# A fused attention and mixture-of-experts kernel: the g column by two matmuls, fewer unused matmuls, a new emission order

## The chip, the cores and the metric

One core of a Trainium2 chip runs the whole program. The metric is the device time of one execution in microseconds. A core has five engines with queues of their own: TensorE (PE in the rows, its weight loads PEld), VectorE (DVE), ScalarE (ACT), GpSimd (POOL) and SyncE (SP). DMAs are issued from SP and POOL here.

## What is computed

Linear attention without softmax for 8 batches of 8 heads, 576 positions and 64 columns, a root-mean-square norm over the 64 columns, and a layer of 8 experts of which each batch takes one, chosen by the mean over its positions:

```python
kv = np.einsum('bhsd,bhse->bhde', k, v)
out = np.einsum('bhsd,bhde->bhse', q, kv)
rms = np.sqrt(np.mean(out * out, axis=-1, keepdims=True) + 1e-06)
x = out / rms * g_norm            # then heads side by side: (8, 576, 512)
...
logits = x.mean(axis=1) @ w_gate  # (8, 8)
e_idx = np.argmax(logits, axis=1)
...
h = np.maximum(x[mask] @ w1[e], 0.0)                     # 512 -> 1024
out[mask] = gate_w[mask, None, None] * (h @ w2[e])       # 1024 -> 512
```

The inputs are the same in every run; the experts drawn are 4, 4, 7, 6, 5, 1, 3, 1 for the batches 0 to 7.

## The kernel before

Every step is a small function, and one long string, `ORDER`, names all steps in the order in which they are emitted: two letters, the batch, then arguments (`m1031` is `m1(0, 3, 1)`). Each engine and each DMA queue executes its instructions in this order and waits at each for its operands; so the string fixes who stands behind whom on every engine. Nothing is rescheduled.

Per batch the steps are these. `lq`, `lk`, `lv` load q, k and v (POOL, converted to f16 on the way; q of batch 0 comes over SP in f32 and is converted by `cq`). `kv` multiplies k and v on TensorE (L230), `kc` and `ks` copy the result. q is transposed by `tr` and `te` (TensorE and a VectorE copy, batches 0 and 1) or by `td` (VectorE, batches 2 to 7). `ou` (batches 0 and 1, L278) and `op` (L265) multiply q with kv, for four groups c, each the even or the odd columns of four heads. `oc` copies the product, `sq` squares it, `sa` adds two squares, `me` sums over the 64 columns with a matmul of ones (L322, L327), `ln` takes the reciprocal root (L334), and `xt` (VectorE, L342) writes x in f16, transposed, times the g column `gcol`, with the sum over the positions as a by-product. `ga` and `gb` (batch 0: `gd`, L369) give the logits, `gc` takes their maximum and its index on VectorE (L382). `g2` (POOL) and `g3` give the gate weight.

The weights of the chosen expert are kept in three slots for w1 and three for w2. `cw` first copies the slot that holds the expert if an earlier batch chose it; `wl` and `wm` (POOL queue) then load w1 and w2 only if no earlier one did. For batch 0 the first half of w1 is loaded in f32 by four DMAs on the SP queue (`wh`, L440), as soon as the index is known, and converted by `wc` (L447); `wl01` loads the other half. The expert itself is sixteen blocks `m1` (L488, four matmuls of 288 columns each) with the relu `re` behind each, five tiles `m2` (L508, L516), the scaling `ev` and the stores `so` (SP).

`du` emits so many matmuls of zeros whose result nobody reads (L351). `ph1` changes the PSUM pools from three double banks and two single ones to two double and four single ones. `cs` sets up the constants. `sg4` makes SP wait for the index of batch 4.

Of the kernel before, what the change touches and what calls it, by code (L numbers as in the profile page):

```python
# [25 lines left out]
wl1 m1050 sq23 re050 m1070 oc231 m1020 re070 m1071 re071 re020 m1021 op20 oc20 sq20 sa201 re021
oc221 m1151 re151 td31 m1171 re171 m1141 m1161 sq22 re161 lv5 lq40 lk4 me20 m1170 re170 m1130
re130 lv4 m1030 ln20 sa211 m1100 re100 m1131 re131 me21 ln21 re030 re141 td30 m1111 kv31 kv30
xt20 xt22 xt23 m1121 re121 kc3 ks30 m1140 re140 xt21 ga2 ks311 cw12 m1150 re150 m1101 re101
m1160 re160 op30 oc301 m1110 re110 oc321 sq32 sq301 gb2 gc2 cw21 g30 m203 op31 sq31 ev031 oc311  # L30
re111 m1120 m202 m200 g21 sq33 sa311 oc33 wl2 sa30 me30 du2 lk5 ev02 ev00 ln30 m201 me31 re120
wm1 cw22 xt30 kv41 ln31 g31 xt31 xt33 m204 ev041 ev011 m211 ev111 kv40 m214 ev141 lq41 xt32 ga3
gb3 gc3 cw31 m213 ev131 m1200 re200 m1241 re241 kc4 ks40 ks411 m1230 kv51 m1201 re201 m1240 td40
re240 m1270 td41 re270 m1210 re210 re230 m1271 m1261 re271 kv50 kc5 ks501 m1250 op40 oc401 sq40
re261 oc42 sq421 m212 ev12 m1221 m1211 re221 re250 op41 sq41 lq50 g22 lq51 td51 sa401 m210 ks511
wl3 m1321 oc41 m1370 me40 oc431 sq431 sa411 td50 re211 re321 re370 m1330 ln40 xt40 m1331 re331
me41 ln41 re330 m1220 m1260 re260 xt43 xt41 re220 op50 m1231 sq52 oc521 xt42 ga4 m1371 re371
m1310 re310 lv6 re231 lk6 kv61 ev101 so10 wm2 oc50 m1340 sq50 gb4 m1320 gc4 lq60 cw41 lq61 kv60
re340 kc6 m1251 re251 m1301 re301 op51 sq51 re320 oc511 sq53 oc53 wl4 cw32 m1311 re311 td61
m1350 re350 g32 m1300 re300 td60 ks61 m223 m1361 re361 sa50 m1351 re351 me50 m1341 re341 m1360  # L40
re360 ln50 xt50 ev23 sa51 me51 ln51 xt52 m220 m224 ev24 ks601 op60 sq60 m222 sq62 oc621 ev22 wm3
ev20 m221 xt51 ev21 so24 oc601 m1451 m1431 op61 re431 xt53 m1411 re411 re451 m1400 re400 oc61
lk7 g23 g33 sq611 sq63 oc63 m1410 m1471 re410 re471 m1430 re430 m232 lv7 g24 ev321 cw42 ga5
m1441 re441 m1470 re470 gb5 m1440 re440 m1420 lq70 lq71 m1401 sa601 me60 ln60 re401 gc5 cw51
re420 m233 ev331 sa611 me61 ln61 kv70 td70 xt62 kv71 kc7 ks71 td71 m1461 re461 g34 so31 m1421
m1460 m1450 re450 re460 m231 re421 xt61 xt63 so01 m230 ks701 ev301 op71 sq71 so04 oc711 so14 wm4
m234 sq73 oc731 m240 op70 oc701 cw52 ev311 ev341 xt60 ga6 sq70 m243 sq72 gb6 ev40 gc6 m242 wl5
m1540 wm5 sa71 ev421 ev431 m241 cw61 sa701 m1541 re541 me70 re540 wl6 ev41 m1501 oc72 m1560
re501 re560 m1571 m1561 re571 m1510 re510 m1550 re550 re561 m1570 m1511 re511 m1520 m1531 re531
m1551 me71 so41 re520 re570 so40 re551 ln70 m1530 m1521 re521 cw62 wm6 m244 m254 re530 ln71 ev44  # L50
m253 g25 g35 ev531 m1500 m1641 re500 re641 so30 m1620 re620 m1661 ev541 so21 so54 re661 m1600
re600 m250 ev501 m1621 re621 xt72 xt71 xt73 xt70 ga7 m1671 re671 gb7 gc7 so11 so00 m1631 m1640
re631 m1630 re630 m1651 re651 m1670 so34 re670 m1601 re601 m252 ev521 re640 m1660 m251 ev511
so20 so50 re660 cw71 wl7 m1741 re741 m1650 re650 m1730 m1761 re761 m1611 re611 m1751 re751 so51
m1700 re700 m1770 cw72 wm7 re730 m1610 re610 re770 m1750 m1721 re721 g26 g36 m1771 re771 m1731
re731 m1710 re710 m1711 m1701 re711 re701 re750 m1760 re760 m1720 re720 m1740 g27 g37 m262 m260
ev60 ev62 m274 m264 m261 ev74 ev61 re740 m271 ev64 so64 so60 so74 m263 ev711 ev631 so61 m272
# [545 lines left out]
```

## Time and profile before

| | |
|---|---|
| three runs | 192.07, 193.81, 194.74 us; median 193.81 |
| profiled execution | 194.13 us, span 192.2 us |
| mean granted TensorE clock | 0.973 |
| TensorE / VectorE / ScalarE / GpSimd busy | 176.0 / 107.9 / 109.0 / 51.7 us |
| DMA | 37.64 MB, mean 196 GB/s |

The span runs from the first to the last instruction; the time of the execution holds 1.9 us more. Busy time is the time in which at least one instruction of the engine runs. In the clock strip one digit stands for 4.8 us and 9 for the full clock of 2.4 GHz. In the windows the columns are the stretch, its length, the busy time of PE, PEld, DVE, ACT and POOL with the number of instructions begun, the granted clock, the mean share of the 16 DMA engines that is busy, and what they wrote in GB/s. A bracket in the timeline says how long the engine had been idle and what ended that.

### The profile page before, as it was taken

The page shows a single profiled execution, that of the slowest core. Times are in us where ns is not written, and L with a number is a line of the kernel's source. Part 1 is how long each engine was busy: PE and PEld are TensorE (multiplying, and loading weights), DVE is VectorE, ACT ScalarE, POOL GpSimd, SP SyncE. Part 2 cuts the span into 40 slices and gives each one's busy share as a digit, 9 for nine tenths or more (in the row PEclk, how much of TensorE's full clock was granted, in tenths as well). Part 3 has the DMA queues.
Part 4 walks back from the last instruction along what each step waited for, and adds up shares of the span by engine and source line. Part 5 has one row for each costly group of instructions (what it writes and reads, how often), then busy time and mean ns, then how long its engine had stood idle before and what let it go on. Part 6 is the DMA issues. An engine that isn't in the chain of part 4 may idle for free.

```text
span 192.2 us, 5276 instructions
## 1 busy us (share of the span) xinstructions
PE 176.0 (92%) x2189; PEld 105.1 (55%) x2189; DVE 107.9 (56%) x229; ACT 109.0 (57%) x241; POOL 51.7 (27%) x68
## 2 busy tenths in 40 slices
PE   7937999789999899999999999979699999999994
PEld 2424435356675355756566466644377575775452
DVE  1135563787798594769949997487433615003211
ACT  2525202789888633979897555665367554880120
POOL 7630029400900750800056901101215004200000
PEclk9995599999999999999999999999999999999999
DMA  5899989999999699899999999999999996600085
GB/s 198 154 212 206 208 151 169 240 207 208 216 204 205 90 204 206 132 205 207 211 234 201 164 202 207 212 258 274 219 211 219 308 284 260 222 0 3 14 314 193
DMA packets 24071, 37.64 MB, mean 196 GB/s; under 512 B 1904, under 2 KB 15984, under 8 KB 23920
## 3 DMA queue, kind: packets, MB, share of 16 engines
q0 software_dynamic: 16992, 25.63, 76.6%
q1 hardware_dynamic: 7056, 11.69, 17.7%
q8 instruction: 17, 0.28, 0.5%
q14 instruction: 6, 0.05, 0.1%
HBM read 61.88 MB, written 9.44 MB: 371 GB/s over the span
## 4 chain that ended last, share of the span: by engine, by line
PE 45%; DMA 29%; ACT 8%; issue 7%; DVE 6%; SPq 1%; POOL 1%; DVEq 0%; POOLq 0%
DMA w<-in_moe_w_dram 18%; PE ps_m L488 17%; PE ps_m L508 17%; DMA vt<-in_v_dram 5%; DMA qf<-in_moe_w_dram 5%; PE ps_d L351 3%; ACT sq L302 2%; ACT hT L496 2%; PE ps_a L230 2%; PE ps_m L516 2%; DVE w L406 2%; PE ps_a L265 1%; ACT ln L334 1%; DVE xT L342 1%; PE ps_a L327 1%
## 5 line engine op out<-in xcount | busy, mean ns | idle before, releaser
L488 PE MATMUL ps_m<-xT,w 128*128 128x288 f16 x512 | 70.2, 286 | 2.6 <-DMA w<-in_moe_w_dram 1.6
L508 PE MATMUL ps_m<-w,hT 128*128 128x512 f16 (+1 forms) x264 | 59.2, 373 | 2.4 <-DMA w<-in_moe_w_dram 1.2
L488 PEld LDWEIGHTS <-w 128*128 128x128 f16 x512 | 48.8, 98 | 19.7 <-issue 2.9
L496 ACT ACTIVATE hT<-ps_m 128x288 f16<-128x288 f32 x128 | 48.3, 419 | 14.9 <-PE ps_m L488 12.6
L508 PEld LDWEIGHTS <-hT 128*128 128x128 f16 x264 | 25.2, 99 | 29.5 <-issue 4.2
L521 ACT ACTIVATE ot<-ps_m,gates 128x512 f32<-128x512 f32 (+1 forms) x19 | 12.8, 677 | 27.2 <-PE ps_m L508 25.3
L342 DVE SCALAR_TENSOR_TENSOR xT<-o,gcol,ln 128x576 f16<-128x576 f32 x32 | 24.8, 808 | 2.1 <-ACT o L308 1.0
L406 DVE COPY w<-w 128x4096 f16 (+1 forms) x14 | 18.4, 1318 | 11.1 <-DMA w<-in_moe_w_dram 6.4
L523 DVE TENSOR_SCALAR ot<-ps_m,gates 128x512 f32<-128x512 f32 (+1 forms) x14 | 9.9, 727 | 20.4 <-PE ps_m L508 19.7
L432 POOL DMA_DIRECT2D w<-in_moe_w_dram x7 | 3.7, 530 | 64.9 <-DMA w<-in_moe_w_dram 22.9
L302 ACT ACTIVATE sq<-ps_a 128x576 f32<-128x576 f32 (+1 forms) x26 | 16.7, 661 | 5.8 <-DVE o L308 2.5
L351 PE MATMUL ps_d<-junk 128*128 128x512 f16 x47 | 17.2, 479 | 2.1 <-DVE eps L165 1.3
L215 DVE STREAM_TRANSPOSE qT<-qt 128x1152 f16<-128x1152 f16 x12 | 16.2, 1365 | 2.8 <-DMA qt<-in_q_dram 2.7
L308 DVE COPY o<-ps_a 128x576 f32<-128x576 f32 x14 | 10.5, 753 | 11.6 <-ACT sq L302 8.2
L334 ACT ACTIVATE ln<-ps_a,eps 128x576 f32<-128x576 f32 x16 | 11.8, 744 | 5.7 <-PE ps_a L322 4.5
L351 PEld LDWEIGHTS <-junk 128*128 128x128 f16 x63 | 6.6, 116 | 12.9 <-issue 9.2
L469 POOL TENSOR_TENSOR lg<-e,lg 128x8 f32<-128x8 f32 x8 | 13.5, 1688 | 0.1
L242 ACT CAST kv<-ps_a 128x256 f16<-128x256 f32 x9 | 3.3, 372 | 16.9 <-issue 11.1
L308 ACT COPY o<-ps_a 128x576 f32<-128x576 f32 x18 | 11.7, 648 | 2.1 <-PE ps_a L265 2.0
L463 POOL DMA_DIRECT2D w<-in_moe_w_dram x8 | 4.7, 587 | 24.8 <-DVE w L406 10.4
L230 PE MATMUL ps_a<-vt,kt 64*64 64x64 f16 x648 | 7.9, 199 | 3.3 <-DMA vt<-in_v_dram 3.3
L230 PEld LDWEIGHTS <-kt 64*64 64x64 f16 x648 | 6.7, 112 | 6.1 <-issue 5.5
(64 smaller groups left out, 135.3 us busy)
## 6 DMA issues: line engine op xcount, KB each, us to landing
w<-in_moe_w_dram POOLq DMA_DIRECT2D x15, 1024.0 KB, 11.5
...
```

The source lines that it names most:

```text
L215: nc.vector.transpose(s["qT"][:, js].rearrange("p j a n -> p (j a n)"), s["q"][:, js].rearrange("p j d -> p (j d)"))
L230: nc.tensor.matmul(pk[64 * o:64 * o + 64, i, c * Dh:(c + 1) * Dh], s["k"][rs, cc, j, :], s["v"][rs, cc, j, :], start=(j == 0), stop=(j == 8))
L302: nc.scalar.activation(t, po, AF.Square)
L308: (nc.scalar.copy if act else nc.vector.tensor_copy)(t, po)
L334: nc.scalar.activation(t.rearrange("p (i n) -> p i n", i=2), s["pm", C][:, :, 0:HS], AF.Abs_reciprocal_sqrt, bias=cs["eps"])
L342: nc.vector.scalar_tensor_tensor(out=s["xT"][:, c, :], in0=s["o", c], scalar=cs["gcol"][:, c % 2:c % 2 + 1], in1=s["ln", c // 2], op0=ALU. ...
L351: nc.tensor.matmul(t, cs["junk"][:, 0:P], cs["junk"], start=True, stop=True)
L406: nc.vector.tensor_copy(w[:, b % 3:b % 3 + 1, :], w[:, ds(s["src"], 1), :])
L469: nc.gpsimd.tensor_tensor(out=s["lg"], in0=cs["e"], in1=s["lg"], op=ALU.pow)
L488: nc.tensor.matmul(ph[:, 0:HS], w1[:, c, c0:c0 + 255:2], s["xT"][:, c, i * HS:(i + 1) * HS], start=(c == 0), stop=(c == NC - 1))
L496: nc.scalar.activation(s["hT"][:, f, i * HS:(i + 1) * HS], s["ph", f, i][:, 0:HS], AF.Relu)
L508: nc.tensor.matmul(po[:, ds_], s["hT"][:, f, c0:c0 + P], s["w2"][:, f, ds_], start=(f == 0), stop=(f == 7))
```

## The change

The g vector, which four DMAs wrote as a column into four groups of 32 partitions, is loaded as one row, four times side by side on one partition; the new step `cg` makes the column from it with two matmuls against a single 1.0 and a VectorE copy. The string ORDER is new from end to end. It holds one block of 16 unused matmuls at the start, ten more between batch 1's kv products and the first expert matmul, one at the end, and none elsewhere; before there were 19 at the start, 37 more up to the first expert matmul, 2 later and 5 at the end. A number of `oc`, `sq`, `sa`, `ks` and `ev` steps change their engine. Both strings are shown up to batch 1's logits, and at their end.

```diff
 ORDER = """
-lk00 lq0 cq01 du1 du2 du16 cs tr02 wg cq00 tr00 lv00 tr01 te00 kv00 du2 te01 kc00 ou01 ou00 sq00
-oc00 lk01 oc011 lv01 kv01 kc01 ou02 sq011 me00 sq02 oc02 ln00 xt00 ou03 sq03 xt01 me01 ln01
-oc031 xt03 gd00 du2 xt02 du2 du2 gd01 du2 du2 du2 gd03 gd02 lq1 du2 du2 du2 gc0 lq21 du2 du1 du1
-du2 du2 ph1 lv1 tr11 lq20 td20 tr12 tr10 td21 lk1 kv11 kv10 te11 lv2 du2 du1 kc1 te10 ou10 oc10
-ou13 du2 sq10 ou12 sq13 oc13 wh00 wc002 oc121 du2 sq121 sa111 wh01 wh10 wc102 wc0241 du2 ou11
-oc111 sq11 sa101 m1010 m1001 wh11 wc1241 wb me11 re001 ln11 xt13 re010 m1000 me10 ln10 m1031
-re031 m1011 re000 wl01 m1061 re061 lk2 m1041 re041 xt10 xt11 xt12 ga1 lq30 m1060 re060 g20 lk3
-lq31 kv21 kv20 kc2 ks20 ks211 m1051 re051 gb1 gc1 cw11 m1040 re040 lv3 re011 wm0 op21 sq21 oc21
...
-ev721 sg4 so72 so71 so44 m270 ev70 so70 m273 ev73 so73 m275 ev751 cw01 du2 du1 du2 so75
+lq0 cs wg lk00 du16 cq01 cq00 tr02 te01 cg tr00 tr01 te00 lv00 kv00 kc00 ou01 oc011 ou00 sq011
+sq00 me00 ln00 lk01 lv01 kv01 kc01 ou02 oc001 xt00 sq02 xt01 oc02 lq1 ou03 sq03 oc031 me01 ln01
+xt03 gd03 gd01 gd00 xt02 gd02 gc0 ph1 tr11 lv1 tr10 te10 tr12 te11 lk1 kv11 kv10 du2 kc1 ou10
+oc101 sq10 lq21 lq20 td20 lv2 ou12 wh00 wh01 lk2 oc12 sq121 du2 wh10 ou13 sq13 oc131 du1 ou11
+sa111 me11 g20 wl01 oc11 sq11 du2 sa10 du1 wc002 lv3 td21 wc0241 ln11 xt13 xt12 du2 m1001 me10
+wc102 m1011 re001 ln10 re011 xt11 wh11 wc1241 lk3 kv21 kv20 kc2 ks20 xt10 ga1 m1000 re000 m1010
+re010 m1031 m1030 ks211 re030 lq31 lq30 m1021 wb re021 m1020 re020 re031 op21 sq23 oc231 wm0 lk4
+gb1 gc1 cw11 m1051 re051 m1040 re040 sq21 oc21 m1050 re050 m1061 m1041 m1060 m1070 op20 oc20
...
+m262 g36 ev62 m260 ev60 m1731 cw72 wm7 re701 m261 ev611 m263 ev631 so61 m270 re731 so51 g37 m271
+ev711 ev70 so70 so60 m272 ev721 so72 m274 ev74 so74 so71 m264 ev64 so64 m275 m273 ev75 so75
+ev731 so73 du1
 """
...
         s["gcol"] = const.tile([P, 2], F32, name="gcol")
-        for h in range(4):
-            nc.sync.dma_start(s["gcol"][32 * h:32 * h + 32],
-                              g_norm.rearrange("(p j) -> p j", j=2))
+        s["grow"] = const.tile([1, 4, Dh], F32, name="grow")
+        nc.sync.dma_start(s["grow"], g_norm.rearrange("(o n d) -> o n d", o=1, n=1)
+                          .to_broadcast([1, 4, Dh]))
...
+        s["one"] = const.tile([1, 1], F32, name="one")
+        nc.vector.memset(s["one"], 1.0)
...
+    def cg():
+        t = psum1()
+        for j in range(2):
+            nc.tensor.matmul(t[:, j:j + 1],
+                             cs["grow"].rearrange("p n d -> p (n d)")[:, j:4 * Dh:2],
+                             cs["one"], start=True, stop=True)
+        nc.vector.tensor_copy(cs["gcol"], t[:, 0:2])
```

## Rows read from the trace of the kernel before

**Rows 1.** Page: TensorE's busy us (share of span, instructions); granted clock by slice.

```profile
PE 176.0 (92%) x2189; PEld 105.1 (55%) x2189; DVE 107.9 (56%) x229; ACT 109.0 (57%) x241; POOL 51.7 (27%) x68
...
PEclk9995599999999999999999999999999999999999
```

**Rows 2.** Windows: busy us (instructions) by engine, granted clock, DMA share, GB/s.

```profile
36.84:44.34 7.50, 6.54 (x112) 4.35 (x113) 6.71 (x16) 6.00 (x14) 0.00 (x0) 1.00 1.21 209
44.34:100.00 55.66, 53.73 (x903) 33.60 (x904) 41.45 (x86) 42.87 (x101) 16.72 (x22) 1.00 1.08 194
100.00:151.50 51.50, 48.48 (x526) 29.52 (x524) 36.12 (x73) 30.56 (x69) 15.57 (x16) 1.00 1.07 222
151.50:188.31 36.81, 36.81 (x258) 23.69 (x259) 8.62 (x21) 16.82 (x41) 3.32 (x4) 1.00 0.53 168
```

**Rows 3.** Timeline, 14 to 37 us: start, us, engine, operation, [idle before <-releaser].

```profile
14.56 1.17 PE L230 MATMUL ps_a<-vt,kt 64*64 64x64 f16 x72 [1.25 <-DMA vt<-in_v_dram]
...
16.20 0.44 PE L278 MATMUL ps_a<-qT,kv 64*32 64x288 f16 x8 [0.47 <-ACT kv L242]
...
16.58 1.14 PE L327 MATMUL ps_a<-sq,ones 128*128 128x288 f16 x4
...
17.76 0.74 ACT L334 ACTIVATE ln<-ps_a,eps 128x576 f32<-128x576 f32 x1 [0.39 <-PE ps_a L327]
...
18.40 0.64 ACT L302 ACTIVATE sq<-ps_a 128x576 f16<-128x576 f32 x1
18.53 0.82 DVE L342 SCALAR_TENSOR_TENSOR xT<-o,gcol,ln 128x576 f16<-128x576 f32 x1 [0.38 <-ACT ln L334]
...
25.59 4.70 PE L351 MATMUL ps_d<-junk 128*128 128x512 f16 x14
...
27.48 2.28 POOL L427 DMA_DIRECT2D w<-in_moe_w_dram  x4 [14.89 <-DVE lg L387]
...
30.13 0.61 PE L198 MATMUL ps_a<-ident,qt 128*128 128x128 f16 x8
...
36.85 1.15 PE L488 MATMUL ps_m<-xT,w 128*128 128x288 f16 x8
```

**Rows 4.** Chain of waits, 14 to 45 us: start, us, what.

```profile
20.01 0.88 PE ps_d L351 x2
...
24.80 0.59 PE ps_d L351 x2
...
25.77 0.18 DVE mx L382
...
29.44 9.44 DMA qf<-in_moe_w_dram
...
44.34 0.36 PE ps_m L375 x2
```

**Rows 5.** Windows, two of the first 30 us; same columns.

```profile
9.60:11.60 2.00, 0.00 (x0) 0.10 (x1) 1.41 (x2) 0.00 (x0) 0.75 (x1) 1.00 1.28 204
...
24.00:30.00 6.00, 5.50 (x23) 2.17 (x22) 3.26 (x7) 0.00 (x0) 2.39 (x5) 1.00 0.89 167
```

**Rows 6.** DMA issues: queue, count, KB each, median us to landing.

```profile
w<-in_moe_w_dram POOLq DMA_DIRECT2D x15, 1024.0 KB, 11.5
...
gcol<-in_g_norm_dram SPq DMA_DIRECT2D x4, 0.2 KB, 5.7
```

**Rows 7.** Groups by line and shape, gate products: busy us, mean ns | idle.

```profile
L369 PEld LDWEIGHTS ps_m<-wg,pl 128*128 128x128 f32 x8 | 1.8, 256 | 0.7 <-issue 0.3 <-DVE xT L342 0.2
...
L369 PE MATMUL ps_m<-wg,pl 128*128 128x8 f32 x8 | 1.4, 269 | 0.0
```

**Rows 8.** Chain of waits, 139 to 173 us; same columns.

```profile
139.90 11.55 DMA w<-in_moe_w_dram
...
159.42 1.73 PE ps_m L508 x8
...
163.36 9.31 PE ps_m L488 x76
```

More of the change, by code (lines that the diff above doesn't have):

```diff
@@ L24 @@
-re031 m1011 re000 wl01 m1061 re061 lk2 m1041 re041 xt10 xt11 xt12 ga1 lq30 m1060 re060 g20 lk3
-lq31 kv21 kv20 kc2 ks20 ks211 m1051 re051 gb1 gc1 cw11 m1040 re040 lv3 re011 wm0 op21 sq21 oc21
[L26 to L57, printed above, removed]
-ev721 sg4 so72 so71 so44 m270 ev70 so70 m273 ev73 so73 m275 ev751 cw01 du2 du1 du2 so75
+lq0 cs wg lk00 du16 cq01 cq00 tr02 te01 cg tr00 tr01 te00 lv00 kv00 kc00 ou01 oc011 ou00 sq011
@@ new lines @@
+gb1 gc1 cw11 m1051 re051 m1040 re040 sq21 oc21 m1050 re050 m1061 m1041 m1060 m1070 op20 oc20
+oc22 re041 re061 re070 re060 wl1 m1160 m1120 re120 re160 sq221 sa21 lv4 m1141 re141 m1161 re161
+m1171 kv30 kv31 m1101 re171 kc3 ks31 sq20 sa20 ks30 td30 m1150 re101 lq41 m1170 re170 me21 ln21
+xt23 lq40 g21 m1121 re121 m1130 re130 m1100 m1151 re151 td31 re100 me20 ln20 m1111 m1071 re071
+re111 m1110 lk5 re150 op30 m1140 xt22 xt20 re140 oc301 m1131 re131 oc321 sq32 sq30 m202 m200
+xt21 cw12 wm1 op31 g30 ga2 gb2 re110 sq31 sq33 ev00 oc331 oc311 ev02 m203 ev031 m214 kv40 kv41
@@ new lines @@
+kc4 ks401 gc2 sa30 me30 cw21 ln30 g31 m210 ev141 lv5 m213 ev101 sa31 me31 ln31 cw22 ks41 td40
+m211 m201 ev011 kv50 kv51 m204 cw01 xt30 ev13 td41 kc5 ks501 op40 oc401 xt32 xt33 sq40 xt31 ga3
+ev111 oc42 sq421 ev041 m212 ev12 wl2 gb3 op41 gc3 cw31 sq41 oc411 m1260 m1271 re271 m1251 re260
+re251 m1241 m1240 m1230 oc43 sa401 sq43 re240 re241 m1231 re231 g22 lq50 lq51 td50 m1200 re200
+sa411 m1220 m1201 re230 me40 re201 m1221 ln40 m1250 re250 re221 re220 m1211 me41 ln41 m1210
+re211 m1261 re261 m1270 re210 ks51 td51 xt43 g32 xt40 xt41 op51 sq51 re270 oc511 sq53 oc531 wm2
@@ new lines @@
+m223 ev23 m222 cw32 ev221 xt42 ga4 op50 oc501 sq501 sq52 m224 wl3 m1330 re330 m1301 re301 ev241
+so24 m1371 re371 m1311 m1350 lq60 m1341 re350 re341 re311 gb4 lv6 lq61 g23 sa501 me50 m1361
+re361 ln50 sa511 gc4 cw41 m1321 re321 m1300 re300 m1310 re310 g33 oc52 m1360 re360 me51 ln51
+m220 ev201 m1331 re331 xt51 m1340 re340 xt53 td60 td61 m1370 sg4 re370 m1351 lk6 kv61 kv60 m1320
+xt52 so01 kc6 re351 re320 ks60 xt50 ga5 m221 wm3 cw42 ev21 ks611 op60 sq60 sq62 oc621 m234 oc601
+gb5 gc5 m231 ev311 op61 sq63 sa611 ev341 m232 ev321 wl4 m233 cw51 ev331 m1431 oc61 sq61 sa601
@@ new lines @@
+so34 m1451 re451 m1450 m1401 g24 g34 re450 re431 lq71 m1411 re411 re401 wm4 m1441 m1440 re440
+re441 m1471 m1461 g25 re461 m1421 oc631 re421 cw52 re471 m1410 re410 m230 ev30 so00 m1430 me61
+ln61 re430 wl5 xt63 g35 m1470 re470 m1420 re420 m244 me60 ln60 xt60 ev441 so44 m243 ev431 m1520
+re520 so10 m1531 re531 so30 m1540 re540 xt61 xt62 ga6 m1550 re550 lq70 m1560 re560 m1570 re570
+m1571 re571 m1551 re551 m1561 re561 td71 td70 gb6 m1400 re400 gc6 lv7 m1460 re460 m1500 re500
+m1510 cw61 m1511 m1541 re541 re511 lk7 kv71 kv70 kc7 m242 m1521 wm5 re510 ks70 ev421 so41 ks71
@@ new lines @@
+op71 sq73 oc73 m1501 re501 sq71 m1530 m241 re521 oc711 re530 op70 oc701 wl6 cw62 wm6 m254 sq701
+g26 m240 sa701 ev411 me70 ev54 so54 ev401 ln70 xt70 sq72 so04 m251 m250 m1651 re651 sa711 me71
+ln71 so14 m1601 re601 so11 m252 ev511 ev501 oc72 xt71 xt72 m1641 re641 ev52 so50 m1621 re621
+m1640 re640 m1610 re610 m1620 re620 xt73 ga7 gb7 m1611 gc7 cw71 g27 m1650 re650 re611 m1630
+re630 m253 ev531 m1671 m1600 re600 so21 so31 so20 so40 m1631 re631 re671 m1660 m1661 re661 re660
+wl7 m1720 m1721 re721 re720 m1740 re740 m1741 re741 m1670 re670 m1750 m1710 re710 re750 m1730
@@ L59 @@
+re730 m1770 re770 m1771 re771 m1711 m1760 re760 m1761 re761 m1700 re700 m1751 re751 re711 m1701
+m262 g36 ev62 m260 ev60 m1731 cw72 wm7 re701 m261 ev611 m263 ev631 so61 m270 re731 so51 g37 m271
+ev711 ev70 so70 so60 m272 ev721 so72 m274 ev74 so74 so71 m264 ev64 so64 m275 m273 ev75 so75
+ev731 so73 du1
 """
@@ L568 @@
                  ln=ln, xt=xt, ga=ga, gb=gb, gd=gd, gc=gc, wl=wl, wm=wm, cw=cw, g2=g2,
-                 g3=g3, du=du, m1=m1, re=re, m2=m2, ev=ev, ph=ph, wg=wg, wh=wh, wc=wc, wb=wb, sg=sg, so=so,
+                 g3=g3, du=du, m1=m1, re=re, m2=m2, ev=ev, ph=ph, wg=wg, wh=wh, wc=wc, wb=wb, cg=cg, sg=sg, so=so,
                  cs=lambda: cs.update(setup()))
```

## The prediction

> **What bounds the kernel now.** I read the page's busy times and clock strip first, then windows over the whole span, the chain of waits, and the first 45 us instruction by instruction. The reader is to see three stretches.
>
> TensorE is busy 176.0 of 192.2 us [rows 1], but not all of that is needed work. From 151.5 us, where the first expert's w1 of batch 6 has just landed, to the last real matmul at 188.31 it is busy 36.81 of 36.81 us [rows 2]: nothing but less TensorE work, or an earlier start of this stretch, moves the end. From 44.34 to 151.5 us it is idle only 55.66 - 53.73 + 51.50 - 48.48 = 4.95 us [rows 2], so a reorder there can win 5 us at most. Ahead of the first expert matmul (36.85 us [rows 3]) the engine is fed with unused matmuls (`du`): 19 before the transposes, then six pairs between and ahead of the last logit products and fourteen more after them [rows 3, 4]. There a chain sets the pace, not throughput: batch 0's last v half arrives, `kv01` starts at 14.56 [rows 3], the logits are read at 25.77 (the max on VectorE), the four quarter loads of w1 go out on SP behind that and the last one lands at 29.44 + 9.44 = 38.88 [rows 4]. Batch 1's logits follow at 44.34 [rows 4].
>
> So the price of the change is read at two places: how much earlier TensorE reaches batch 1's logits (`gb1`), and whether the 144 us behind that stay as dense as they are.
>
> **The new g column.** Four DMAs of 0.2 KB (5.7 us to landing [rows 6]) become one row DMA, two f32 matmuls with one column and a VectorE copy of 128x2. No row shows a matmul of contraction 1. From below it costs nothing; from above, by the gate products, which are f32 too and have two records each, two of them take 2 x 2 x (0.256 + 0.269) = 2.1 us if loads and matmuls do not overlap [rows 7]. I take the gate products' form at half of that, 1.0 us. It stands on TensorE between `tr02` and `tr00`, where the engine has no work from 9.60 to 11.60 us [rows 5] while it waits for v, so the cover is 2.0 us plus what the shorter first block leaves. The row is issued by 2 us and, with the old landing time of 5 to 7 us, is there at about 8. Were it 3 us late, `tr00`, `te00` and `ou01` would follow and the cost would be about 1 us. I count 0, bound 1.
>
> SP issues three DMAs fewer ahead of wg, which nobody needs before the logits: nothing. `cs` now stands ahead of `lk00`, so POOL builds the identity (0.5 us) before the first k half; the v half behind it keeps its place, and v is what TensorE waits for. Nothing.
>
> **Batch 0 up to its logits.** Two things differ. First a loss: `me00` now stands ahead of `kv01` on TensorE. It needs the square of group 1's copy (copy on ACT, then square on DVE), ready near 14.8 by my estimate (products at 13.4, then two steps of 0.64 to 0.8 us), and takes 1.14 us at the half clock [rows 3]; `kv01` starts at about 15.85 instead of 14.56, so 1.3 us late. Behind it by rows: `kv01` 1.17, its cast with the wait for it 0.47, `ou02` 0.44, two squares of 0.64, `me01` 1.14, `ln01` 0.74, two xT of 0.82 [rows 3] and a last gate product of 0.5 [rows 7]: 15.85 + 1.17 + 0.47 + 0.44 + 1.28 + 1.14 + 0.74 + 1.64 + 0.5 = 23.2, with hand-overs 23.3. Second the gain: before, the gate products wait behind the pairs of unused matmuls that run from 20.01 to 25.39 [rows 4]; now nothing stands between them. The logits are read at about 23.3 instead of 25.77: 2.4 us earlier. The 1.3 us loss is inside that.
>
> **Batch 1 up to the first expert matmul.** Before, fourteen unused matmuls (4.70 us from 25.59) stand between the logits and batch 1's transposes at 30.13 [rows 3]. They are gone. Are the operands there? Between 24 and 30 us the DMA share was down to 0.89 [rows 5]: all that had been asked for, the last of it v of batch 2, had landed by some 27 us. The new queue puts q, v and k of batch 1 ahead of q and v of batch 2, 1.18 MB or 6 us at 194 GB/s [rows 2], so they are there well before. Transposes can start at 23.5, 6.6 us earlier. From there to the first expert matmul it was 36.85 - 30.13 = 6.7 us; the new order puts `me11`, the transposition `td21` and the copies of ou in front, and TensorE may still be at half clock, which adds 1.2 us to transposes and kv. I add up 9.5 us: first expert matmul at 33.0 instead of 36.85.
>
> It can't all be kept. Blocks 2 and 3 need the last two w1 quarters. SP issues them 2.4 us earlier; if they again take 9.44 us, the last lands at 36.5, is cast in 0.6 us, and `m1031` starts at 37.2 where it could have at 36. From there TensorE has about 2.2 us to `gb1`: 39.4 against 44.34, a gain of 4.9 us. Up to `gb1` both orders hold the same TensorE work (one expert block of four matmuls less, 32 small `op21` matmuls more). POOL now issues `lk2` before it waits for the expert index; before, it sat 14.89 us in that wait with `lk2` behind it [rows 3]. So the engines do not run dry, but the w1 quarters share with the rest of v and k of batch 2. By bytes: 1.05 MB at half of 209 to 222 GB/s [rows 2] takes 9.5 to 10 us, so the quarters are no later than assumed, or up to 2.5 us later if they get less. I allow 0.3 us, bound 2.5.
>
> The Trainium skill (Trainium Kernel Development and Optimization, Key Constraints) says that the SP, ACT and POOL queues run on the same 16 DMA engines and interleave. No row of before separates the queues; by that rule the quarters get no more than their share although SP issues nothing else then, which speaks for the upper bound, 192.2 us in the sum where I have 190.0.
>
> **The rest of the order.** I counted TensorE's work between each batch's logits and its first use of the weights in both orders. With 0.49 us for an expert block (76 matmuls in 9.31) and 1.73 for a second-layer tile [rows 8] it goes for batch 2 from 15.4 to 15.7 us, for 3 from 13.0 to 14.3, for 4 from 14.8 to 17.1, for 5 from 17.4 to 17.7, for 6 from 15.8 to 16.1: no tighter, against 11.5 us that such a load needs [rows 6]. Squares, copies and scalings that change engine add 0.7 us to ACT and 1.4 to POOL and take 2.9 from DVE over the whole kernel: nothing. I keep the 4.95 us of idle time; the bounds are 2 and 8. But with TensorE 4.6 us ahead the transfers must be too. w1 of batch 6, issued at 139.90, took 11.55 us and TensorE's stretch without idle time begins as it lands [rows 2, 8]; the DMA share from 44 to 151 us is 1.07 to 1.08 [rows 2] where 1.21 to 1.28 is reached [rows 2, 5], so a tenth of some 107 us, over 10 us, is not used. I charge 0.5 us, bound 3.
>
> **Sum**, in the profiled run's own time (194.13 us, span 192.2): -4.9 + 0.3 + 0.5 = -4.1, so 190.0. That run lies 0.3 us above the median of 193.81, so 189.7.
>
> **Rivals.** *Transfers set the pace.* What is won early is waited away at a weight load, at the latest at batch 6. For it: TensorE's only waits over 1 us after 100 us are on w, and that load decides the last 36.81 us [rows 2, 8]. Against it: the unused tenth. Then only the time in which they ran dry is won, from 24 to 30 us (1.21 - 0.89) / 1.21 x 6 = 1.6 us [rows 2, 5]: 192.2 us.
>
> *The new order is denser too.* Half of the 4.95 us of idle time and the charges go: 186.5 to 187. For it: the loads' lead above. Against it: in-order queues meet new waits as easily as they lose old ones.
>
> *Slower: the clock stays low into the expert work.* Thirty unused matmuls fewer run ahead of the first expert matmul. Before, the granted clock fell to the lower level by the fourth slice (14.4 us), after the idle 9.60 to 11.60, and was back at full in the sixth (24.0 us), four us into the pairs of unused matmuls, and stayed [rows 1, 4, 5]. A block of four expert matmuls takes 0.57 us at 2.4 GHz (two in 1.15 [rows 3]) and would take twice that at 1.2. Half a dozen slow blocks with their stalls cost 3 us and leave the time within 2%; the gain is gone at 4.1 us of matmul work run slow, and at 8 us, close to all sixteen blocks of batch 0, the kernel is slower by 2%: 198 us. Against it: from 23.5 us TensorE has hardly a gap, and the last six unused matmuls stand close to the first block.
>
> The page TensorE: Matmul & The Clock Gate (the Trainium skill, Why this matters for your kernels) says that idle stretches between bursts of matmuls bring the clock back to half. By that rule the fall after the first block comes again, as the trace of before has it; whether the expert work starts slow no row shows.
>
> **How the numbers follow.** The forecast has a chance of 0.50 with its own range from 187.6 to 191; the denser order 0.15, transfers 0.22, the low clock 0.13. A difference under 2%, 189.9 to 197.7 here, can hardly be told from no change. About 0.35 of the forecast's half lies below 189.9; with the denser order, faster is 0.50. The rest of the forecast and the transfers make 0.38 for the same. Slower is 0.12. The range for 8 in 10 reaches from the denser order to a mild form of the low clock: 186.3 to 194.0.
>
> **What would show it.** Logits of batch 0 read at 23 to 24 us, not 25.8; transposes of batch 1 right behind; first expert matmul near 33; last w1 quarter cast by 37.5; batch 1's logits at 39 to 40. The clock strip at half from about 13 to no later than 35 us. TensorE without idle time from batch 6's first expert matmul on, which starts near 147. If batch 1's logits are early and the end is not, transfers or new waits took it back; if the first expert blocks last 1 us each, it was the clock; if batch 0's logits are not early, my reading of the pairs of unused matmuls was wrong.

## The result and the profile after

The changed kernel takes 188.24 us (median of four executions, 186.37 to 189.98; a fifth on record took 192.44) against 193.53 us of the kernel before on the same chip (192.07 to 194.74): a ratio of 0.964 with a 95% interval from 0.952 to 0.975. Unedited, it was timed on two more chips: 190.97 against 194.59 us, ratio 0.991 [0.979, 1.003] (E0), and 187.75 against 194.68 us, ratio 0.970 [0.964, 0.975] (E11). The ratios leave out executions more than 1.5% above the fastest of their kernel, so they are not the ratios of these medians (0.973, 0.981, 0.964). On E0's chip alone the gain is not clear of the noise. The forecast was 189.7 us in a range from 186.3 to 194.0. The execution that is profiled took 189.98 us (span 188.1) and is the slowest of its four, so the traces of E0 (span 187.8) and E11 (185.6) stand beside it.

First the page of after: TensorE's busy us (share, instructions) and the granted clock by slice of 4.7 us.

```profile
PE 167.1 (89%) x2157; PEld 104.7 (56%) x2157; DVE 107.6 (57%) x231; ACT 108.2 (58%) x239; POOL 55.9 (30%) x69
...
PEclk9998585799999999999999999999799999999999
```

TensorE is busy 8.9 us less than before [rows 1] in a span that is 4.1 us shorter. The clock strip shows two stretches at half clock in the first 40 us where before had one, and a third short one near 134 us.

The timeline of after on TensorE, 10 to 35 us (start, us, engine, operation, idle before and what ended it), answers [rows 3]:

```profile
10.18 0.77 PE L240 MATMUL ps_a<-vt,kt 64*64 64x64 f16 x72 [0.51 <-DMA vt<-in_v_dram]
...
13.07 0.65 PE L337 MATMUL ps_a<-sq,ones 128*128 128x288 f16 x4 [1.19 <-ACT sq L312]
13.65 0.78 PE L240 MATMUL ps_a<-vt,kt 64*64 64x64 f16 x72
...
18.65 1.88 PE L379 MATMUL ps_m<-wg,pl 128*128 128x8 f32 x8 [1.69 <-DVE xT L352]
20.38 1.87 PE L208 MATMUL ps_a<-ident,qt 128*128 128x128 f16 x16
...
29.35 0.64 PE L332 MATMUL ps_a<-sa,ones 128*128 128x288 f16 x2 [1.44 <-DVE sa L324]
29.79 2.34 PE L361 MATMUL ps_m<-junk 128*128 128x512 f16 x5
31.92 1.16 PE L498 MATMUL ps_m<-xT,w 128*128 128x288 f16 x4
```

Batch 0's gate products run in one piece and batch 1's transposes stand right behind them at 20.38, where before they began at 30.13 [rows 3]. The first expert matmul starts at 31.92 (36.85 before), and its block of four lasts 1.16 us: half clock.

The windows of after, with the columns of [rows 2]; the first ends and the second begins with batch 1's logits:

```profile
31.92:38.98 7.06, 6.99 (x140) 4.50 (x138) 4.48 (x14) 5.09 (x13) 4.36 (x7) 0.80 1.19 217
38.98:100.00 61.02, 58.27 (x868) 37.81 (x852) 50.29 (x100) 45.01 (x104) 25.78 (x27) 1.00 1.10 198
100.00:151.00 51.00, 47.88 (x571) 28.72 (x571) 27.64 (x59) 30.39 (x68) 9.58 (x10) 0.97 1.05 217
151.00:183.39 32.39, 32.39 (x236) 21.20 (x233) 8.96 (x21) 14.59 (x36) 2.42 (x3) 1.00 0.45 167
```

Batch 1's logits come 44.34 - 38.98 = 5.36 us earlier than before [rows 4]. Behind them TensorE is idle 2.75 + 3.12 = 5.87 us, against 4.95 before [rows 2]. Where that time lies is in the chain of waits of after, from 24 us on (start, us, what):

```profile
24.20 11.87 DMA qf<-in_moe_w_dram
...
74.44 1.76 issue
...
112.53 20.64 DMA kt<-in_k_dram
133.21 0.83 PE ps_a L240 x72
134.03 3.41 PE ps_m L518 x8
```

The last quarter of w1 takes 11.87 us and sets the pace to 36.07, as the 9.44 us did before [rows 4]; in this execution TensorE hardly waits for it, as it is busy 6.99 of 7.06 us up to the logits, partly at half clock. In E11, whose clock is back earlier, the wait is seen (timeline, TensorE):

```profile
36.74 1.89 PE L497 MATMUL ps_m<-xT,w 128*128 128x288 f16 x14 [1.17 <-ACT w L456]
```

At 74.44 TensorE stands still inside a step. At 133.21 it has waited for the k of batch 7, and the eight second-layer matmuls behind that take 3.41 us, where [rows 8] has 1.73: half clock again.

### The profile page after: what moved, and what is told of

It reads as the page before. It is cut to its first block, busy times and chain, and to the rows that moved or that the text cites. A ratio compares the mean times of both kernels' runs of the same rounds, so it can differ in the third digit from the quotient of the medians.

```text
span 188.1 us, 5205 instructions
## 1 busy us (share of the span) xinstructions
PE 167.1 (89%) x2157; PEld 104.7 (56%) x2157; DVE 107.6 (57%) x231; ACT 108.2 (58%) x239; POOL 55.9 (30%) x69
## 3 DMA queue, kind: packets, MB, share of 16 engines
HBM read 61.88 MB, written 9.44 MB: 379 GB/s over the span
## 4 chain that ended last, share of the span: by engine, by line
PE 59%; DMA 25%; DVE 5%; ACT 4%; issue 3%; SPq 1%; POOL 1%; POOLq 0%
PE ps_m L518 26%; PE ps_m L498 22%; DMA kt<-in_k_dram 11%; DMA qf<-in_moe_w_dram 6%; DMA vt<-in_v_dram 4%; DMA w<-in_moe_w_dram 4%; PE ps_m L526 4%; PE ps_a L240 2%; PE ps_a L275 2%; DVE qT L225 1%; DVE kv L262 1%; DVE xT L352 1%; SPq L450 1%; PE ps_a L332 1%; PE ps_m L379 1%
## 5 line engine op out<-in xcount | busy, mean ns | idle before, releaser
L498 PE MATMUL ps_m<-xT,w 128*128 128x288 f16 x512 | 68.7, 289 | 0.5 <-DMA w<-in_moe_w_dram 0.3
L518 PE MATMUL ps_m<-w,hT 128*128 128x512 f16 (+1 forms) x264 | 60.3, 380 | 0.0
L498 PEld LDWEIGHTS <-w 128*128 128x128 f16 x512 | 49.7, 99 | 17.1 <-issue 1.6
L531 ACT ACTIVATE ot<-ps_m,gates 128x512 f32<-128x512 f32 (+1 forms) x21 | 14.2, 682 | 25.8 <-PE ps_m L518 19.3
L479 POOL TENSOR_TENSOR lg<-e,lg 128x8 f32<-128x8 f32 x8 | 15.0, 1873 | 18.7 <-DVE lg L394 9.7
L533 DVE TENSOR_SCALAR ot<-ps_m,gates 128x512 f32<-128x512 f32 (+1 forms) x12 | 8.6, 726 | 18.9 <-PE ps_m L518 18.8
L318 ACT COPY o<-ps_a 128x576 f32<-128x576 f32 x20 | 12.7, 648 | 1.6 <-PE ps_a L288 0.9
L318 DVE COPY o<-ps_a 128x576 f32<-128x576 f32 x12 | 8.9, 749 | 4.5 <-ACT sq L312 3.7
L324 POOL TENSOR_TENSOR sa<-sq 128x576 f16<-128x576 f32 x5 | 7.0, 1410 | 12.2 <-ACT sq L312 8.3
L262 DVE COPY kv<-kv 32x256 f16<-32x256 f16 x16 | 5.3, 330 | 7.9 <-ACT kv L252 7.6
## 6 DMA issues: line engine op xcount, KB each, us to landing
w<-in_moe_w_dram POOLq DMA_DIRECT2D x15, 1024.0 KB, 11.5
```

Source lines behind the costliest of these rows:

```text
L318: (nc.scalar.copy if act else nc.vector.tensor_copy)(t, po)
L479: nc.gpsimd.tensor_tensor(out=s["lg"], in0=cs["e"], in1=s["lg"], op=ALU.pow)
L498: nc.tensor.matmul(ph[:, 0:HS], w1[:, c, c0:c0 + 255:2], s["xT"][:, c, i * HS:(i + 1) * HS], start=(c == 0), stop=(c == NC - 1))
L518: nc.tensor.matmul(po[:, ds_], s["hT"][:, f, c0:c0 + P], s["w2"][:, f, ds_], start=(f == 0), stop=(f == 7))
L531: nc.scalar.mul(dst, src, gate)
```

## The experiments

The theory: the end follows batch 1's logits, these follow the last quarter of w1, and this follows batch 0's logits, so the unused matmuls and the order together give the gain. The rivals: transfers later set the pace and take the gain back, or the low clock does, or one part of the change alone is the gain.

**The unused matmuls alone, the g row alone, both, in the old order.** E1 takes the 26 unused matmuls between the gate products and batch 1's transposes out of the kernel before:

```diff
-oc031 xt03 gd00 du2 xt02 du2 du2 gd01 du2 du2 du2 gd03 gd02 lq1 du2 du2 du2 gc0 lq21 du2 du1 du1
-du2 du2 ph1 lv1 tr11
+oc031 xt03 gd00 xt02 gd01 gd03 gd02 lq1 gc0 lq21 ph1 lv1 tr11
```

> The kernel before, its order kept, without the 26 unused matmuls between the first gate product of batch 0 and batch 1's transposes. Theory 1 (they stand in the chain to the first expert matmul): batch 0's logits read at about 23.1 instead of 25.8 us, batch 1's transposes right behind, batch 1's logits at 40 to 41 instead of 44.3, time about 190 us. Rival A (they kept the clock up and paid for themselves): the chain is as early, but kv, q times kv and the first expert blocks of batch 1 run at the lower clock, and the time is 192.5 to 194 us. Rival B (the new emission order makes the difference): batch 1's logits may be early, but the later order gives it back, 192.5 to 194 us with TensorE idle for 8 us or more behind them.

Measured: 193.92 us, ratio 1.004 [0.989, 1.018]. The logits of batch 0 come at 23.21 instead of 25.77, the first expert matmul at 32.29 instead of 36.85, and nothing is won: the last quarter is cast at 39.33 (38.90 before) and batch 1's logits come at 45.09 (44.34 before). Windows of E1, columns as in [rows 2]:

```profile
34.00:36.00 2.00, 1.64 (x12) 1.09 (x12) 0.00 (x0) 1.21 (x3) 0.00 (x0) 1.00 1.16 230
36.00:38.00 2.00, 0.28 (x3) 0.24 (x4) 1.10 (x2) 0.00 (x0) 0.00 (x0) 1.00 1.20 216
38.00:40.00 2.00, 0.38 (x4) 0.08 (x2) 0.02 (x1) 0.67 (x2) 0.00 (x0) 0.96 1.21 208
```

TensorE, busy 0.28 and 0.38 of 2 us, waits for the quarters, which the queues behind an earlier start have to share with the loads of batches 1 and 2 (DMA share 1.16 to 1.21). So the unused matmuls before cost nothing that can be measured by themselves in the old order: their time was covered by that load. The granted clock also fell to half from 39.84 to 43.25 us, which may be part of why the logits are 0.75 us late.

E7 gives the kernel before the g row and the step `cg` (behind `te01`), nothing else; E10 has both edits, E1's and E7's.

```diff
-lk00 lq0 cq01 du1 du2 du16 cs tr02 wg cq00 tr00 lv00 tr01 te00 kv00 du2 te01 kc00 ou01 ou00 sq00
+lk00 lq0 cq01 du1 du2 du16 cs tr02 wg cq00 tr00 lv00 tr01 te00 kv00 du2 te01 cg kc00 ou01 ou00
+sq00
```

> The kernel before with the g column as one row, two matmuls and a copy, nothing else. Theory 3 (the four DMAs' 8-byte packets hold back the first k and v loads, as the run with four DMAs in the new order suggests, 2.4 us there): v's first half is there at 9.5 to 10.2 instead of 11.6 us, the logits of batch 0 are read at 23.5 instead of 25.8, batch 1's logits at about 42.3 instead of 44.3; time 0 to 2 us below the kernel before, as much as the later weight loads leave. Rival (in the old order v is late for another reason, the k load's place): v as before, time within 0.5 us.

> The kernel before, its old order, with both other parts of the change: the g row and no unused matmuls between the first gate product and batch 1's transposes. Theory 4 (in the old order the last w1 quarter lands some 14 to 16 us after the logits, since it shares with a full POOL queue; each part alone left batch 1's logits where they were): logits of batch 0 at 21, last quarter at 36 to 37, batch 1's logits at 41 to 42.5, the old order then runs on with 6 to 8 us of loss as before, last matmul at 185 to 186.5 us, time 2 to 3 us below the kernel before. Rival B (order): batch 1's logits stay at 44 and the time is that of the kernel before or 1 us less. Rival 1 (unused matmuls and g alone make the gain): batch 1's logits at 39 to 40 and the time of the changed kernel.

Measured: E7 192.17 us, ratio 0.993 [0.986, 0.999]; E10 191.98 us, ratio 0.989 [0.982, 0.995]. In E7 `kv00` starts at 9.56 us instead of 11.61 and `kv01` at 12.56 instead of 14.56: the g column did cost 2 us. The logits gain only 1.2 us (24.61) and the last quarter 0.3 us (38.59); on the way TensorE stands still for 1.39 us at 14.98, where the trace shows no wait (see the gap further down). In E10 the last quarter is there as early as in after, yet batch 1's logits come at 41.55. Chain of waits of E10:

```profile
25.20 10.53 DMA qf<-in_moe_w_dram
35.75 0.63 ACT w L456
36.38 0.05 issue
36.43 3.98 PE ps_m L497 x18
40.41 0.71 PE ps_a L239 x72
41.11 0.60 PE ps_m L497 x4
41.71 0.12 PE ps_m L384 x2
```

The window of E10 from the last quarter to the logits, columns as in [rows 2]:

```profile
35.75:41.55 5.80, 5.13 (x96) 3.49 (x95) 4.22 (x11) 4.70 (x11) 0.00 (x0) 0.71 1.22 206
```

Between the quarter and the logits the old order has 22 expert matmuls and a kv product left, 5.8 us from 35.75 to 41.55; the new order has put that work elsewhere, and from 36.09 to 38.98 it needs 2.9 us. Not all of the difference is the order: E10's clock is at half from 36.32 to 39.73 us, worth up to 1.7 us, while after's is back at full from 34.80. But the kernel before, at full clock, needs 5.4 us for the same stretch (38.90 to 44.34). E11, the changed kernel timed beside E10, takes 187.75 us against 191.98, and the intervals of their ratios lie apart ([0.964, 0.975] and [0.982, 0.995]): this is the part that the order brings.

**The unused matmuls put back into the new order.** E2 inserts the same 26 into the kernel after, at the matching places:

```diff
-xt03 gd03 gd01 gd00 xt02 gd02 gc0 ph1 tr11
+xt03 gd03 du2 du2 du2 gd01 gd00 xt02 du2 du2 du2 gd02 du2 du2 du2 gc0 du2 du1 du1 du2 du2 ph1 tr11
```

> The changed kernel with 26 unused matmuls put back between batch 0's gate products and batch 1's transposes, 12 ahead of the logits and 14 behind. Theory 1: batch 0's logits 2 to 3 us later than 20.6, batch 1's logits 4 to 5 us later than 39.0, time 192 us, so the changed kernel plus 4. Rival A (clock): the clock is full at the first expert matmul, which takes back 2 us or more: changed kernel plus 1 to 2. Rival B (order): the changed kernel plus 0 to 1, because the later order has room.

Measured: 194.13 us, ratio 0.997 [0.981, 1.013]. Timeline of E2 on TensorE:

```profile
18.83 3.15 PE L361 MATMUL ps_d<-junk 128*128 128x512 f16 x6
...
22.48 3.15 PE L361 MATMUL ps_d<-junk 128*128 128x512 f16 x6
...
25.71 5.77 PE L361 MATMUL ps_d<-junk 128*128 128x512 f16 x14
...
40.20 1.17 PE L498 MATMUL ps_m<-xT,w 128*128 128x288 f16 x4
```

The logits of batch 0 are at 25.90, batch 1's at 46.55, 7.5 us later than in the same chip's run of after (39.07, E0). With the g row in all four cases the two parts stand like this:

| with the g row | old order | new order |
|---|---|---|
| with the 26 unused | 0.993 (E7), logits of batch 1 at 44.04 | 0.997 (E2), 46.55 |
| without | 0.989 (E10), 41.55 | 0.964, 0.991, 0.970 (after), 38.95 to 39.07 |

Neither part gives more than about 1% alone; together they give 2 to 4% by the medians of three chips. E10 and E11 were timed side by side and differ clearly. E2 and E0 were too (194.13 and 190.97 us), but their intervals overlap, so what the 26 cost in the new order is shown at the front and not in the time. In E2 it is not the last quarter that decides: it lands at 37.42 us, nothing waits for it, and batch 1's logits are late by TensorE's own queue, the 14 unused matmuls behind batch 0's logits included. The span of E2's profile is only 2.7 us longer than E0's (190.5 against 187.8), not 7.5: nearly 5 us of a loss at the front are made up behind it. E2 has no wait over 0.43 us for the k of batch 7, where E0 waits 2.63 us. That fits a later bound by transfers.

**The g column by four DMAs in the new order.** E3:

```diff
+            nc.sync.dma_start(s["gcol"][32 * h:32 * h + 32],
+                              g_norm.rearrange("(p j) -> p j", j=2))
...
-sq00 ... tr02 te01 cg tr00
+sq00 ... tr02 te01 tr00
```

> The changed kernel with the g column written by four DMAs as before, without the row, the two matmuls and the copy. Theory 1 (the two matmuls stand in idle time, and the four DMAs cost nothing): within 0.5 us of the changed kernel, v's first half arrives near 10.1 us as there. Rival C (the 128 packets of 8 bytes delay the first loads): v's first half arrives at 11 to 11.6 us, batch 0's logits 1 to 1.5 us later, time plus 1 to 1.5 us.

Measured: 189.16 us, ratio 0.980 [0.967, 0.992], while the unedited kernel beside it (E0) had 0.991 [0.979, 1.003]: no difference that can be measured in the end, but a clear one at the front. Windows of E0 and then of E3, columns as in [rows 2]:

```profile
4.00:6.00 2.00, 2.00 (x10) 0.83 (x9) 0.00 (x0) 0.00 (x0) 2.00 (x4) 1.00 1.03 337
6.00:8.00 2.00, 0.76 (x5) 0.17 (x3) 1.05 (x2) 1.15 (x1) 1.76 (x2) 1.00 1.28 192
```

```profile
4.00:6.00 2.00, 2.00 (x7) 0.69 (x6) 0.00 (x0) 0.00 (x0) 2.00 (x4) 1.00 0.81 289
6.00:8.00 2.00, 1.75 (x18) 0.98 (x17) 1.05 (x2) 1.15 (x1) 1.81 (x2) 1.00 0.75 103
```

While the 128 pieces of 8 bytes are under way the engines move 103 GB/s instead of 192, `kv00` starts at 12.31 instead of 9.93 and batch 1's logits come at 41.05 instead of 39.07. Both spans are 187.8 us: E3 too waits for the k of batch 7, 2.56 us. That k lands 1 us later than in E0 (133.8 against 132.8 us), but the clock stays at full behind it, which it doesn't in E0. So the 2 us at the front are not seen at the end.

**The order of `me00` and `kv01`.** E4 puts `me00 ln00` back behind `kv01 kc01`:

```diff
-sq00 me00 ln00 lk01 lv01 kv01 kc01 ou02
+sq00 lk01 lv01 kv01 kc01 me00 ln00 ou02
```

> The changed kernel with me00 and ln00 of batch 0 behind kv01 and its cast. If the second v half is there before me00 ends at 13.4 us, as the prediction charged with 1.3 us, kv01 starts at 12 to 12.7 instead of 13.41 and batch 0's logits come 0.5 to 1.3 us earlier than 20.32. If v is what kv01 waits for, it starts at 13.4 again and the logits are no earlier, or later by the norm that now stands behind.

Measured in one execution: 187.29 us. `kv01` starts at 12.63 instead of 13.41 to 13.65, but the logits come at 20.43, no earlier than in the unedited kernel (20.16 to 20.56). So the exchange makes `kv01` 0.8 to 1.0 us later, but the 1.3 us that the prediction charged do not reach the logits.

**The ten late unused matmuls.** E8 removes them from after:

```diff
-kv11 kv10 du2 kc1 ... sq121 du2 wh10 ... oc131 du1 ou11 ... sq11 du2 sa10 du1 wc002 ... xt12 du2 m1001
+kv11 kv10 kc1 ... sq121 wh10 ... oc131 ou11 ... sq11 sa10 wc002 ... xt12 m1001
```

> The changed kernel without the ten unused matmuls between batch 1's kv products and the first expert matmul; the first block of 16 stays. If they keep the clock up (rival A of the prediction), the first expert blocks run at 1.2 GHz and the clock comes back later than 34.6 us, batch 1's logits at 40 to 42 instead of 39.1. If they only fill gaps, batch 1's logits come at 38.5 to 39.2 and the clock comes back at the same time.

Measured in one execution: 189.02 us. Windows of E8 up to its logits of batch 1:

```profile
20.78:30.36 9.58, 5.12 (x124) 3.35 (x123) 6.73 (x14) 3.83 (x8) 3.83 (x5) 0.68 1.19 222
30.36:36.49 6.13, 5.33 (x89) 3.21 (x90) 4.05 (x8) 3.12 (x6) 5.65 (x7) 0.50 1.19 235
36.49:39.77 3.28, 3.28 (x51) 2.02 (x49) 2.22 (x7) 3.20 (x9) 0.00 (x0) 0.80 1.21 208
```

The granted clock stays at 0.50 until the last quarter is there, and it is still low behind it (0.80), so batch 1's logits come at 39.77 instead of 38.98. The late unused matmuls are worth 0.8 us there in this one execution, 0.4 of it because the quarter is there 0.4 us later (36.49 against 36.09). TensorE works from 31.82 us on without a wait, at half clock until 37.80, so here the clock is the bound; but the last quarter, cast by 37.11, would have held a faster TensorE too. From that cast to the logits E11 needs 2.3 us and E8 2.7.

**Is the k of batch 7 the bound?** Two trials. In E5, lv5 goes ahead of wm1 on POOL, to fill a stretch from 60 to 63 us in which the DMA engines have little to do; in E9 the kv products of batch 7 move behind `m242`, `m1521` and `m1501`, so that TensorE comes to the wait later. E11 is the unedited kernel beside E9.

```diff
-m1110 lk5 re150 op30 ... m210 ev141 lv5 m213
+m1110 lk5 lv5 re150 op30 ... m210 ev141 m213
```

```diff
-re511 lk7 kv71 kv70 kc7 m242 m1521 wm5 re510 ks70 ev421 so41 ks71 op71 sq73 oc73 m1501 re501 sq71
-m1530 m241 re521 oc711
+re511 lk7 m242 m1521 wm5 re510 ev421 so41 m1501 re521 kv71 kv70 kc7 re501 m1530 ks70 m241 ks71 op71
+sq73 oc73 sq71 oc711
```

> The changed kernel with v of batch 5 asked for ahead of batch 1's w2 instead of behind it (its conditional load waits on POOL for a copy of the slot, 3.5 us, while the DMA share falls to 0.28 in 60 to 63 us). Theory 2 (transfers give back part of the early gain: everything behind that dry spell comes late, and at batch 7's k TensorE waits 2.6 us, after which its clock is at half for 3.4 us): the dry spell is filled by 2.8 us of transfer, batch 7's k lands before it is wanted, the clock stays up there, and the last matmul ends at 179 to 181 us in the trace instead of 183.06; time 3 us below the changed kernel. Rival (the wait at batch 7's k comes from its own late issue behind w1 of batch 5 and from the stores): the wait stays above 1.5 us and the end moves by less than 1.5 us.

> The changed kernel with batch 7's kv products behind m242, m1521 and m1501 (2.7 us of TensorE work) instead of ahead of them, the casts and products that hang on them moved along. Theory 2 (half of the early gain is lost in the wait at batch 7's k, 2.6 us, and in 3.4 us of half clock behind it): the wait is below 0.5 us, the clock strip stays full between 100 and 150 us, and the last matmul ends 2.6 to 4.3 us earlier than in the changed kernel, at 179 to 180.5 us; time 2 to 4 us below the changed kernel beside it. Rival (the transfers set the pace behind that place too): the wait turns up at the next load, w1 of batch 6, wanted near 141 us, and the end moves by less than 1 us.

> The changed kernel without an edit, so that the edits run beside it are compared on the same chip. Expected: 186.4 to 190 us, batch 0's logits read near 20.6 us, batch 1's logits multiplied near 39.0 us. One more question is put to its trace: in the first trace TensorE waits 2.82 us for batch 7's k near 130 us. If that wait belongs to the order, it is there again; if it belongs to that execution, it is not.

> The changed kernel once more, unedited, as the partner on the same chip of the run with batch 7's products later. Expected: 188 to 191 us, the wait at batch 7's k between 0.5 and 3 us: it is the longer, the earlier TensorE gets there, since k lands at 132 to 133 us in every trace so far.

Measured: E5 189.44 us, ratio 0.967 [0.952, 0.983]; E9 188.02 us, ratio 0.966 [0.960, 0.972], against 0.970 [0.964, 0.975] for E11. Neither is measurably better than the unedited kernel (E5 has none timed beside it); both missed the 2 to 4 us that were hoped for. E0 (190.97) and E11 (187.75) lie just outside what was expected of them. E5's dry stretch, windows of E0 (60 and 63 us) and then of E5:

```profile
60.00:63.00 3.00, 3.00 (x112) 1.98 (x111) 2.17 (x6) 2.18 (x6) 2.98 (x3) 1.00 0.28 48
63.00:66.00 3.00, 3.00 (x16) 1.37 (x14) 2.92 (x4) 2.41 (x5) 2.98 (x3) 1.00 1.03 151
```

```profile
60.00:63.00 3.00, 3.00 (x112) 2.01 (x111) 2.18 (x7) 2.18 (x6) 3.00 (x2) 1.00 1.16 199
63.00:66.00 3.00, 3.00 (x16) 1.34 (x15) 2.92 (x4) 2.48 (x5) 2.98 (x3) 1.00 0.46 52
```

The hole (share 0.28) is filled and opens again 3 us later (0.46). In E0 POOL stands 3.45 us at wm1, which loads nothing since batch 1 draws the expert of batch 0, and issues lv5 behind it at 60.97 us. In E5 lv5 has gone before, and POOL issues nothing of weight until wl2 at 63.36, where E0 has it at 63.77. The k of batch 7 was no earlier: its products start at 133.87 us. In E9 the wait for k is gone, and another has come 5 us behind it (timeline of E9's profile, an execution at 189.13 us, above its median):

```profile
133.10 0.78 PE L239 MATMUL ps_a<-vt,kt 64*64 64x64 f16 x72
...
138.21 0.75 PE L274 MATMUL ps_a<-qT,kv 32*32 32x288 f16 x32 [1.62 <-DVE o L317]
```

The product `op71` now waits 1.62 us for a copy on VectorE that frees its PSUM, and the clock falls to half behind it too (139.50 to 142.92 us). So that one wait is not a bound that can be taken away alone.

**The same gap, two clocks.** Windows of E0 and then of E11, the same kernel:

```profile
75.00:78.00 3.00, 1.83 (x16) 1.38 (x15) 2.39 (x5) 1.46 (x4) 0.41 (x1) 1.00 1.13 212
78.00:81.00 3.00, 3.00 (x27) 2.41 (x25) 2.94 (x6) 2.68 (x9) 3.00 (x5) 1.00 1.09 182
...
132.00:135.00 3.00, 2.17 (x77) 1.28 (x78) 0.85 (x4) 0.69 (x2) 0.00 (x0) 0.84 1.12 242
135.00:138.00 3.00, 3.00 (x41) 1.17 (x40) 0.02 (x1) 0.69 (x1) 0.00 (x0) 0.59 1.11 220
```

```profile
75.00:78.00 3.00, 1.77 (x10) 1.12 (x10) 2.40 (x5) 1.18 (x2) 0.41 (x1) 0.79 1.12 210
78.00:81.00 3.00, 3.00 (x18) 1.97 (x17) 2.31 (x3) 1.88 (x5) 3.00 (x5) 0.64 1.09 186
...
132.00:135.00 3.00, 2.58 (x82) 1.57 (x83) 0.87 (x4) 1.05 (x4) 0.70 (x1) 1.00 1.10 267
135.00:138.00 3.00, 3.00 (x51) 1.75 (x49) 0.76 (x1) 2.65 (x6) 0.00 (x0) 1.00 1.13 227
```

Both have a gap near 74.4 us (1.78 and 1.84 us). Behind it E11 runs at 0.64 to 0.79 of the clock and E0 at 1.00. E0 so reaches the k of batch 7 some 1.4 us earlier, waits 2.63 us for it and then falls to 0.59; E11 waits 0.80 us and does not fall. `kv71` starts at 132.83 and 132.42: what E11 lost at 75 us was covered by the wait. Their spans of 187.8 and 185.6 us are apart by these 0.4 us and by the half clock behind E0's wait, 1.7 us. The profiles of this order at 189 to 190 us (after, E0, E3, E8) have waits for that k of 2.6 to 2.8 us, those at 187.3 to 187.6 us (E4, E11) 0.6 and 0.8 us. In E5 TensorE waited 1.9 us and its clock fell twice, in an execution at 190.67 us. This is one trace of each; only the pair E0 and E11 is worked out in full.

Where the gap lies depends on how many instructions TensorE has ahead of it, not on the step. Timeline of after, and then of E2 and E8:

```profile
76.20 0.30 PE L275 MATMUL ps_a<-qT,kv 32*32 32x288 f16 x2 [1.76 <-issue]
```

```profile
83.30 0.46 PE L275 MATMUL ps_a<-qT,kv 32*32 32x288 f16 x28 [1.67 <-issue]
```

```profile
76.70 1.51 PE L497 MATMUL ps_m<-xT,w 128*128 128x288 f16 x11 [0.60 <-issue]
```

In after the gap is behind the 30th of the step's 32 matmuls. In E2, with 26 matmuls more ahead of it, it is behind the 4th, 7 us later; in E8, with ten fewer, ten matmuls further on. In all nine traces of the new order 1,114 matmul records stand ahead of it (1,115 in E3), and it ends 1.33 to 1.47 us after a packet of 16,384 bytes has landed on the queue that the page lists as q8, instruction: in after at 74.82, in E2 at 81.91 us. The stops of 1.39 and 1.50 us near 15 us in E7 and E10 are alike: they end 1.2 to 1.5 us behind the first such packet, seven packets and 1,792 matmuls and weight loads earlier, 256 to a packet. So TensorE most likely waits there for its own next instructions; no run tried to move that.

## Why the prediction came out right

**The size and the place of the gain: right.** Forecast: batch 1's logits at 39.4, 4.9 us earlier; measured 38.98 and 5.4. Forecast for the run's time 190.0 us; measured 189.98 in the profiled execution, 188.24 in the median. The first half of the route is shown: the pairs of unused matmuls held back the gate products (logits of batch 0 at 25.90 in E2, 20.56 in after), and with earlier logits the quarters of w1 go out earlier. That the last quarter then holds back batch 1's logits is seen in E11 (1.17 us); in E2 it is not (37.42 against 46.55), and in E1 earlier logits brought no earlier quarter. That 190.0 and 189.98 agree to the hundredth is luck: the terms below are off by 2 to 3 us with both signs, and the other executions of the kernel took 186.4 to 192.4 us.

**The g column: counted as nothing, worth 2 us at the front.** The matmuls were priced well enough: four records in 0.63 us from 8.04 us on, and a copy of 0.16, in time that TensorE had free. What the step missed is what it took away. It called SP's three DMAs fewer "nothing", since nobody needs wg early; but the small pieces held back the v loads of another queue (E3, E7). The change in the end that this brings is 0.7% in the old order (E7, [0.986, 0.999], hardly clear of 1) and not measurable in the new (E3).

**The exchange of `me00` and `kv01`: charged 1.3 us, costs the logits nothing** (E4). `kv01` started at 13.65, not 15.85: 2 us of that from the earlier v, and the sum of squares ran while TensorE would have waited for v anyhow, 1.07 us in E4. With these two terms the logits of batch 0 came at 20.56, not 23.3. Two misses of one sign, 2.7 us in all, that the next step swallowed: from batch 1's transposes to the first expert matmul I had added up 9.5 us, and it took 11.5 (20.38 to 31.92).

**The last quarter of w1: 36.5 forecast, 36.07 measured, by other terms.** It started 2.8 us earlier than I had it and took 11.87 us instead of 9.44. The allowance was 0.3 us with a bound of 2.5; the upper bound was the truth. The rule of the Trainium skill (Trainium Kernel Development and Optimization, Key Constraints) that SP's and POOL's transfers interleave on the same engines fits these traces, which do not part the queues: the last quarter took 7.89 us at a DMA share of 0.89 (E2), 9.44 at 1.07 (before) and 11.87 at 1.18 (after). E1 shows what it can do: there it ate the whole 4.6 us by which the first expert matmul was earlier.

**The clock: a mild form of the rival.** Forecast: at half from about 13 to no later than 35 us. Measured, by the times at which the granted clock changes: lower from 17.7 to 24.6 us, and again from 28.0 to 34.8, the second time within a stretch from 25 to 30 us in which TensorE is busy 2.43 of 5 us. The first blocks did last 1.16 us. They cost little, because the last quarter is there only at 36.07 us: E11, at full clock from 32.38, reaches batch 1's logits at 38.95, after at 38.98. These two falls go the same way as the rule in TensorE: Matmul & The Clock Gate (the Trainium skill, Why this matters for your kernels): idle stretches between bursts bring the clock back to half. The gap of 1.76 us at 74.44 did not bring it down in after.

**The rest of the order: the right amount, the wrong place.** I kept 4.95 us of idle time and charged 0.5 for transfers. Measured in after: 5.87 us, and the 3.41 - 1.73 = 1.7 us of half clock behind the wait for k. My count of TensorE's work went only over the weight loads, which are hardly a wait any more (0.4 us); I did not count the k and v loads that moved behind them. The k of batch 7 is issued at 112.53, behind a w1, and takes 20.64 us. This is the transfer rival, at another place than batch 6's weights and at a part of its price: it took back 0.9 + 1.7 = 2.6 of the 5.4 us in after's and E0's kind of execution. All the same the last real matmul ends 5.1 us earlier (183.39 against 188.47) and the span is 4.1 us shorter, since what follows takes 1 us more. Of the 2.3 us between 5.1 and 5.4 - 2.6, two unused matmuls fewer in that stretch are 0.6, and the rest I can't place.

**Batch 6's expert** was to start near 147 us with no idle time behind. Its first matmul is at 147.90 us, and TensorE is busy without a gap from 137 us on: right, with a margin.

**What stays open.** Why TensorE's instructions, if it is these that it waits for near 74.4 us, come late there and not behind the other packets of that queue. And why the clock falls behind that gap in E4, E5 and E11 and not in the other traces. A kernel without the gap would tell what it costs; none was run.
